# Batch 0 of an attention + FFN kernel: FFN1 of quad 0 placed ahead of quad 1's, in other PSUM banks; one load moved, one square moved to ScalarE

## The chip, the cores and the metric

One core of a Trainium2 chip. The metric is the device time of one execution in microseconds, the median over the runs. Besides it, every run has a span: the time from the first to the last record of the core's engines. Each ratio below is of runs in the fast state, made in the same rounds on the same chip.

## The reference

```python
def _attn_ref(q, k, v):                      # q, k, v: (8, 12, 448, 64)
    S = q.shape[2]
    scores = np.matmul(q, k.transpose(0, 1, 3, 2)) / np.sqrt(q.shape[-1])
    attn = np.maximum(scores, 0.0) ** 2 / S
    return np.matmul(attn, v)

def _moe_ref(x, w_in, w_out, alpha):         # x: (3584, 768); w_in: (768, 2048); w_out: (2048, 768)
    h = x @ w_in
    g = np.maximum(h, 0.0) + alpha * np.minimum(h, 0.0)
    return g @ w_out
```

The attention output, with its heads side by side, is x. All is float32 outside; the kernel computes with bfloat16 operands.

## The kernel before

Heads are taken four at a time: a "quad" is four heads of one batch, and three quads make one batch. A quad's scores come in seven chunks (`j` from 0 to 6). Each chunk is four matmuls on 64 x 64 quadrants of TensorE, a relu out of PSUM, and a square (two chunks per instruction on VectorE; a seventh chunk alone is the "single" square). Then follows the product with v (`attnv`), whose result is copied to `xT`. FFN1 (`ffn1`) needs all three quads of a batch: inputs `km` 0 and 1 come from quad 0, 2 and 3 from quad 1, 4 and 5 from quad 2.

PSUM is divided into two double buffers (`sc_ps`) and four single banks (`mm_ps`) that rotate. Score chunks use either; FFN1 accumulators use single banks.

```python
    sc_ps = pool("scps", 2, **PSUM)          # tiles [128, 2, 512] float32
    mm_ps = pool("mmps", 4, **PSUM)          # tiles of one bank

    def attnv(n, js=range(NJ), space=sc_ps, apart=False):
        if js[0] == 0:
            if space is mm_ps:
                av_ps[n] = [mm_ps.tile([128, 512], F32, ...) for _ in range(2)]
            elif apart:                      # each half in a double buffer of its own
                av_ps[n] = [sc_ps.tile([128, 2, 512], F32, ...)[:, 0] for _ in range(2)]
            else:
                av_ps[n] = sc_ps.tile([128, 2, 512], F32, ...)
        ...
        for j in js:
            a = att.pop((n, j))
            for r in range(2):
                for s in range(2):
                    nc.tensor.matmul(half[r][64 * s:64 * s + 64, :S], ...)
        ...                                  # batch 0: half 0 copied by ScalarE, half 1 by VectorE (g > 0)

    def ffn1(b, ff, kms=range(KM)):
        if kms[0] == 0:
            hps[ff] = mm_ps.tile([128, S], F32, ...)
        ...                                  # one matmul per km
        nc.scalar.activation(neg, ps, ACTF.Relu, scale=-1.0)
        nc.vector.scalar_tensor_tensor(gT..., neg, beta..., ps, ALU.mult, ALU.add)

    for n in range(NG):                      # batch 0
        last = n == NG - 1
        for j in range(NJ):
            ...
            if j == 2 or j == (4 if last else 5):
                scores(n, j, "both", mm_ps)
            else:
                scores(n, j, "act")
            ...
            if j == 3 and n > 0:
                attnv(n - 1, space=mm_ps)
            ...
            if last and j > 4:
                ffn1(0, j - 5, range(0, 4))
            if last and j == 6:
                ffn1(0, 2, range(0, 4))
        if n == 0:
            load_bf16(2)                     # k, q, v of quad 2
            load_w_in(0, 512)                # four transfers
            load_w_in(512, 1024)
            load_w_in(1024, 2048)
            load_bf16(3)
    ...
    squares(single=nc.vector)
    attnv(2, range(0, 4), apart=True)
    attnv(2, range(4, NJ))
    ffn1(0, 3, range(0, 4))
    ...
    for ff in range(4):
        ffn1(0, ff, range(4, KM))
```

Below, AV1 and AV2 are `attnv` of quads 1 and 2, and "step 4" of FFN1 is its `ff` 4.

## Time and profile before

| | before |
|---|---|
| time, median of the first 3 runs (range) | 390.79 us (390.65 to 391.74) |
| TensorE busy | 379.5 us of a 389.6 us span |
| TensorE's waits after 20 us | 0.38 + 0.21 us |
| AV1's first matmul | 19.74 us |
| AV1's first matmul to the first FFN1 matmul after AV2 | 6.56 us |
| AV1's first matmul to the first FFN2 matmul | 25.66 us |
| first FFN2 matmul to the end of the span | 344.21 us |

### The profile page before, as it was taken

What the parts mean: (1) busy time and instruction counts of PE and PEld (TensorE: products, weight loads), DVE (VectorE), ACT (ScalarE), POOL (GpSimd) and SP (SyncE); (2) the same over time, 40 slices, a digit from 0 to 9 for tenths busy, and PEclk for the clock granted to TensorE, in tenths of its full rate; (3) what the DMA queues carried; (4) which work ended last, traced back from release to release, by engine and by line L of the source; (5) the groups of instructions that cost most, each with busy time, mean ns of one, the idle gap of its engine ahead of it and who ended that gap; (6) DMA issues with size and microseconds to landing.
All of it is one profiled execution on the core that took longest, in us unless ns stands there. A gap on an engine that the chain in (4) does not pass through costs nothing.

```text
span 389.6 us, 7873 instructions
## 1 busy us (share of the span) xinstructions
PE 379.5 (97%) x3210; PEld 214.8 (55%) x3210; DVE 253.2 (65%) x336; ACT 215.5 (55%) x361; POOL 74.9 (19%) x89
## 2 busy tenths in 40 slices
PE   6799999999999999999999999999999999999996
PEld 4345556545655456645665456654566545655564
DVE  4986877687687757766675666777676376726411
ACT  5965767464566656664473645756565366624200
POOL 7654000052251114201221012301030000000000
PEclk9999999999999999999999999999999999999999
DMA  8999997894995519825494354937253220130033
GB/s 163 191 209 204 204 216 264 235 300 100 259 258 182 126 65 240 222 65 164 94 260 150 67 164 98 278 126 174 29 91 87 70 47 2 42 81 2 0 82 81
DMA packets 64755, 55.43 MB, mean 142 GB/s; under 512 B 35776, under 2 KB 60496, under 8 KB 64720
## 3 DMA queue, kind: packets, MB, share of 16 engines
q1 hardware_dynamic: 53504, 44.78, 44.7%
q0 software_dynamic: 10976, 9.96, 16.1%
q8 instruction: 25, 0.41, 0.4%
q10 hardware_dynamic: 240, 0.20, 0.2%
q14 instruction: 10, 0.08, 0.1%
HBM read 45.62 MB, written 11.01 MB: 145 GB/s over the span
## 4 chain that ended last, share of the span: by engine, by line
PE 93%; ACT 2%; DMA 2%; DVE 1%; POOL 1%; issue 0%; POOLq 0%; DVEq 0%
PE hps L255 37%; PE ops L271 37%; PE avh L223 7%; PE sc L156 6%; PE sch L156 3%; DMA qe<-in_q_dram 2%; PE ops L294 1%; PE av L223 1%; PE tps L131 1%; ACT rl L185 1%; DVE at L196 1%; ACT xT L232 0%; POOL ke L357 0%; POOL ke L355 0%; POOL qe L355 0%
## 5 line engine op out<-in xcount | busy, mean ns | idle before, releaser
L255 PE MATMUL hps<-xT,w_in_sb 128*128 128x448 bf16 x768 | 149.2, 353 | 0.6 <-ACT xT L232 0.4
L271 PE MATMUL ops<-w_out_sb,gT 128*128 128x384 bf16 x864 | 145.8, 326 | 0.0
L263 DVE SCALAR_TENSOR_TENSOR gT<-neg,beta_sb,hps 128x448 bf16<-128x448 f32 x128 | 85.7, 679 | 58.3 <-ACT neg L262 57.5
L271 PEld LDWEIGHTS <-gT 128*128 128x128 bf16 x864 | 83.4, 98 | 61.2 <-issue 7.9
L255 PEld LDWEIGHTS <-w_in_sb 128*128 128x128 bf16 x768 | 74.0, 98 | 72.5 <-issue 5.5
L262 ACT ACTIVATE neg<-hps 128x448 f32<-128x448 f32 x128 | 69.1, 546 | 63.7 <-PE hps L255 63.6
L185 ACT ACTIVATE rl<-sc 128x896 bf16<-128x896 f32 x87 | 77.1, 923 | 44.1 <-PE sc L156 44.0
L196 DVE TENSOR_TENSOR at<-rl 128x1792 bf16<-128x1792 bf16 x80 | 85.7, 1113 | 2.1 <-ACT rl L185 0.9
L106 DVE COPY osb<-ops 128x384 f32<-128x384 f32 x30 | 16.7, 557 | 45.6 <-PE ops L271 45.6
L163 ACT ACTIVATE rl<-sch 128x448 bf16<-128x448 f32 x81 | 41.6, 550 | 4.7 <-PE sch L156 4.6
L106 POOL CAST kb<-kraw 128x896 bf16<-128x896 f32 x16 | 18.8, 1178 | 114.5 <-DMA kT<-kb 55.9
L156 PE MATMUL sc<-qT,kT 64*64 64x448 bf16 x456 | 36.1, 355 | 3.1 <-ACT rl L185 1.4
L223 PE MATMUL avh<-at,vb 64*64 64x448 bf16 x588 | 34.4, 350 | 0.4 <-DVE at L196 0.4
L156 PEld LDWEIGHTS <-kT 64*64 64x64 bf16 x672 | 21.8, 106 | 19.6 <-issue 13.2
L104 ACT COPY osb<-ops 128x384 f32<-128x384 f32 x24 | 11.4, 476 | 36.0 <-PE ops L271 36.0
L223 PEld LDWEIGHTS <-vb 64*64 64x64 bf16 x672 | 25.7, 106 | 9.8 <-issue 5.2
L183 DVE TENSOR_SCALAR rl<-sc 128x896 bf16<-128x896 f32 x27 | 29.4, 1089 | 0.6 <-PE sc L156 0.6
L106 POOL CAST vb<-vraw 128x896 bf16<-128x896 f32 x16 | 15.9, 991 | 36.8 <-PE avh L223 36.7
L106 POOL CAST qb<-qraw 128x896 bf16<-128x896 f32 x16 | 16.6, 1040 | 32.3 <-DMA qT<-qb 28.0
L156 PE MATMUL sch<-qT,kT 64*64 64x448 bf16 x216 | 22.5, 355 | 0.0
L165 DVE TENSOR_SCALAR rl<-sch 128x448 bf16<-128x448 f32 x27 | 16.8, 622 | 2.8 <-PE sch L156 0.8
L238 DVE TENSOR_SCALAR xT<-avh 128x448 bf16<-128x448 f32 x19 | 11.9, 624 | 7.7 <-PE avh L223 7.7
(59 smaller groups left out, 98.4 us busy)
## 6 DMA issues: line engine op xcount, KB each, us to landing
out_dram<-osb SPq DMA_DIRECT2D x54, 192.0 KB, 2.8
qraw<-in_q_dram SPq DMA_DIRECT2D x19, 448.0 KB, 5.3
kraw<-in_k_dram SPq DMA_DIRECT2D x18, 448.0 KB, 4.4
vraw<-in_v_dram SPq DMA_DIRECT2D x18, 448.0 KB, 6.1
w_out_sb<-in_moe_w_out_dram POOLq DMA_DIRECT2D x2, 1536.0 KB, 20.0
w_in_sb<-in_moe_w_in_dram POOLq DMA_DIRECT2D x8, 192.0 KB, 8.7
w_in_sb<-in_moe_w_in_dram POOLq DMA_DIRECT2D x4, 384.0 KB, 9.8
vb<-in_v_dram POOLq DMA_DIRECT2D x6, 224.0 KB, 9.6
```

Source lines behind the costliest of these rows:

```text
L106: eng.tensor_copy(o, i)
L156: nc.tensor.matmul(half[r][64 * c:64 * c + 64, :S], kT[n][64 * r:64 * r + 64, j, c, :], qT[n][64 * r:64 * r + 64, :, c, :], start=True, st ...
L163: nc.scalar.activation(rl[:, r], half[r][:, :S], ACTF.Relu)
L165: nc.vector.tensor_scalar(rl[:, r], half[r][:, :S], 0.0, None, ALU.max)
L183: nc.vector.tensor_scalar(rl, ps[:, :, :S], 0.0, None, ALU.max)
L185: nc.scalar.activation(rl, ps[:, :, :S], ACTF.Relu)
L196: nc.vector.tensor_tensor(a, t, t, ALU.mult)
L223: nc.tensor.matmul(half[r][64 * s:64 * s + 64, :S], vb[n][64 * r:64 * r + 64, s, j, :], a[64 * r:64 * r + 64, s], start=(j == 0), stop=(j ...
L255: nc.tensor.matmul(ps, w_in_sb[:, km // 2, km % 2, bass.ts(ff, 128)], xT[b][:, km // 2, km % 2, :], start=(km == 0), stop=(km == KM - 1))
L262: nc.scalar.activation(neg, ps, ACTF.Relu, scale=-1.0)
L263: nc.vector.scalar_tensor_tensor(gT[b // 2][:, ff, (b % 2) * S:(b % 2) * S + S], neg, beta_sb[:, ff:ff + 1], ps, ALU.mult, ALU.add)
L271: nc.tensor.matmul(ps, gT[sb][:, ff, bass.ts(c, 128)], w_out_sb[:, ff, bass.ts(hf, 384)], start=(ff == 0), stop=(ff == KF - 1))
```

## The change

Its intent is to remove TensorE's wait for a PSUM bank before the first FFN1 matmul. Chunk 4 of quad 2 no longer takes two single banks, so that FFN1's first accumulators find the banks of chunk 2 free. The matmuls of quad 0, which is ready early, then go ahead of those of quad 1. The first columns of w_in, now needed earlier, are loaded ahead of quad 2's v, and the single square goes to ScalarE.

```diff
@@ batch 0, scores
-            if j == 2 or j == (4 if last else 5):
+            if last and j == 4:
+                scores(n, j, "both")
+            elif j == 2 or j == 5 and not last:
                 scores(n, j, "both", mm_ps)
@@ batch 0, FFN1
-            if last and j > 4:
-                ffn1(0, j - 5, range(0, 4))
+            if last and j == 4:
+                ffn1(0, 0, range(0, 2))
+                ffn1(0, 1, range(0, 2))
+            if last and j == 5:
+                ffn1(0, 0, range(2, 4))
+                ffn1(0, 1, range(2, 4))
             if last and j == 6:
                 ffn1(0, 2, range(0, 4))
         if n == 0:
-            load_bf16(2)
+            load_bf16(2, "kq")
             load_w_in(0, 512)
+            load_bf16(2, "v")
             load_w_in(512, 1024)
@@ after batch 0's scores
-    squares(single=nc.vector)
+    squares(single=nc.scalar)
     attnv(2, range(0, 4), apart=True)
```

## The prediction

> **What bounds the kernel now.** I first read the page: busy shares, slices, chain.
>
> ```profile
> span 389.6 us, 7873 instructions
> PE 379.5 (97%) x3210; PEld 214.8 (55%) x3210; DVE 253.2 (65%) x336; ACT 215.5 (55%) x361; POOL 74.9 (19%) x89
> ...
> PEclk9999999999999999999999999999999999999999
> ...
> PE 93%; ACT 2%; DMA 2%; DVE 1%; POOL 1%; issue 0%; POOLq 0%; DVEq 0%
> ```
>
> TensorE is busy for 97% of the span and carries 93% of the chain, at full clock. All TensorE idle time together is about 10 us (389.6 minus 379.5). The change touches only batch 0, so I took TensorE's waits from 18 to 40 us:
>
> ```profile
> PE sc L156 <- DVE qT L106: 0.6, 1, 0.6
> PE sc L156 <- ACT rl L185: 0.6, 2, 0.3
> PE hps L255 <- ACT xT L232: 0.4, 1, 0.4
> PE hps L255 <- DVE gT L263: 0.2, 1, 0.2
> ```
>
> The first two lie before 19.6 us, ahead of the changed code. Only the other two, 0.6 us, are in its reach. From 30 us to the end TensorE waits for nothing. The TensorE timeline gives the order (columns: start, duration, engine, line, operation, idle before with its releaser):
>
> ```profile
> 19.74 1.52 PE L223 MATMUL avh<-at,vb 64*64 64x448 bf16 x28
> 21.06 0.42 PE L156 MATMUL sch<-qT,kT 64*64 64x448 bf16 x4
> 21.25 0.42 PE L156 MATMUL sc<-qT,kT 64*64 64x448 bf16 x4
> 22.05 0.94 PE L255 MATMUL hps<-xT,w_in_sb 128*128 128x448 bf16 x4 [0.38 <-ACT xT L232]
> 22.92 0.38 PE L156 MATMUL sc<-qT,kT 64*64 64x448 bf16 x4
> 23.23 1.69 PE L255 MATMUL hps<-xT,w_in_sb 128*128 128x448 bf16 x8
> 24.85 1.52 PE L223 MATMUL av<-at,vb 64*64 64x448 bf16 x28
> 26.30 2.44 PE L255 MATMUL hps<-xT,w_in_sb 128*128 128x448 bf16 x12
> 28.96 0.35 PE L255 MATMUL hps<-xT,w_in_sb 128*128 128x448 bf16 x1 [0.21 <-DVE gT L263]
> ```
>
> The first FFN1 matmul (hps) follows chunks 4 (sch) and 5 (sc) of quad 2 and starts at 22.05, when ScalarE has copied quad 1's half 0 out of avh (xT, 21.37 to 22.00). It needs only quad 0, ready since 16.6 (the copies at 15.66 and 16.10 took 0.54 each). It waits for its bank: the four single banks rotate (avh takes two, sch of chunk 4 two), so the next tile gets a bank that avh still holds. That is the wait the change attacks.
>
> **What the Trainium skill says.**
> 1. "Perfetto Trace Analysis", Optimization Strategy: find the gaps of the engine that bounds the regime and what semaphore ends them. The trace agrees that this is the place to look, but the gaps here come to 0.6 us in 389.6.
> 2. "ScalarE: Activation LUTs", What ACT_TABLE_LOAD costs: an ACTIVATE with immediate scale and bias takes 186 + 0.833 N ns. For N = 896 that is an estimate of 932 ns; the trace has 923 (relu) and 950 (the Squares it already runs). Agrees. It counts a load for a switch of table sets; the trace shows one load in all, with Relu, Copy and Square running after it, so I add none.
> 3. "DMA: Bandwidth & Descriptors", Issuing engines are not separate DMA queues: all transfers run on the same 16 engines. Moving v behind w_in thus adds no bandwidth, it changes an order. The trace agrees so far as POOL's issues wait in turn for earlier landings.
> 4. "PSUM — Partial Sum Buffer", The four PSUM rules: one matmul output stays within a 2 KiB bank. Chunks of 448 float32 columns are 1,792 bytes, one bank each, as the pools have it; the trace has no row on the bank size itself.
>
> **The change part by part.**
>
> (a) *Banks.* Chunk 4 moves from two single banks to one double score buffer. The first two hps tiles then take chunk 2's banks, whose relus ended at 20.75 (ScalarE, 20.15 + 0.60) and 21.06 (VectorE, 20.44 + 0.62). Chunk 4 takes the buffer of chunk 1, whose relu is over by about 20.3; chunk 5 that of chunk 3 (over at 20.57 + 0.99 = 21.56); chunk 6 now that of chunk 4, whose VectorE half ended at 22.50 + 0.61 = 23.11.
>
> (b) *Order.* The build shows the new TensorE order: chunk 4, four hps matmuls of quad 0 (ff 0 and 1), chunk 5, four of quad 1, chunk 6, four for ff 2, attention of quad 2 (AV2). The same matmuls as before, so no work is removed. Two durations from the timeline: a chunk between FFN1 groups takes 23.23 - 22.92 = 0.31; four FFN1 matmuls up to the next chunk take 22.92 - 22.05 = 0.87. Walking from the end of AV1 at 21.06:
> - chunk 4 at 21.06, hps quad 0 at 21.37,
> - chunk 5 at 22.24 (21.56 is past),
> - hps quad 1 at 22.55; its first input is ready at 22.00, its second at 21.97 + 0.62 = 22.59, and it comes second, at about 22.75,
> - chunk 6 at 23.42 (23.11 is past),
> - hps ff 2 at 23.73, AV2 at 24.60.
>
> Against 24.85 that is 0.25 us: the stall of nearly 0.5 (21.56 to 22.05 in starts) goes, and one more switch between 64-row chunks and full FFN1 matmuls (0.31 instead of the 0.19 that chunk 4 took, and some 0.06 at the end of an FFN1 group, plus rounding) takes about half of it back.
>
> (c) *The wait that takes its place.* AV2 puts its second half into the buffer of chunk 6, so its third matmul needs chunk 6's relu. Elsewhere in the trace a relu starts 0.45 after its chunk (16.07 to 16.52), takes 0.92, and releases TensorE 0.04 later: 1.41 us. Before, eight FFN1 matmuls followed chunk 6 and hid this (22.92 + 1.41 = 24.33, before 24.85; ScalarE in fact ended at 24.27). Now only four follow: 23.42 + 1.41 = 24.83. The third matmul of AV2 stood at about 24.95 before (two at 0.05, from 28 in 1.45). **The gain shrinks from 0.25 to 0.12 us.**
>
> (d) *The last square.* It leaves VectorE (0.62 us, 25.04 to 25.66) and costs 0.95 on ScalarE. There it starts when chunk 6's relu is over, about 24.82, ending near 25.77. AV2's first use of it is its 25th matmul, 24.83 + 22 x 0.052 = 25.97. VectorE still squares chunks 4 and 5 until 25.12, for the 17th matmul at 25.56. ScalarE's next task, the xT copy, begins after AV2, above 26.2. Off the path by about 0.2 us: worth nothing, costing nothing.
>
> (e) *v behind w_in.* POOL's waits show one eight-deep order: issue n waits for landing n - 8. From it, quad 2's v landed at 17.2 and the four first w_in pieces by about 18.0, 18.9, 20.2 and 21.2. The first hps now starts at 21.37 and its second matmul needs the last piece: in the old order that is a margin of about 0.3 us. In the new order w_in moves one place up (some 2 us earlier), and v lands about 21.2, needed at 24.6. It is insurance for (a), not a gain itself.
>
> (f) *The second gap.* The fifth hps tile takes the first one's bank, after its last matmul (ending 27.62), neg (0.55), gT (0.69) and hand-overs, to 28.96. The order and banks there are the same in the new build, so this 0.2 stays, moved with the rest.
>
> **Sum:** 0.38 us of attacked wait, about 0.13 back to switching, about 0.13 to the relu of chunk 6: **0.12 us gained of 390.8.**
>
> **Rivals.**
> - *All of the gap is gained.* If relu 6 ends sooner or chunk 6 is issued sooner than I walk it, up to 0.4 us, 390.4. For it: the stall is real and on the chain. Against it: the relu's 1.41 us is longer than the 0.31 + 0.87 of work now beside it.
> - *A wait takes its place wholly.* The square on ScalarE is 0.33 longer than on VectorE, with 0.2 of slack; if it slips, or chunk 5's or 6's buffers come free late, AV2 stalls for 0.2 to 0.5: 390.8 to 391.1. Against it: each hand-over above is met by 0.1 us or more.
> - *A transfer becomes the bound.* The last w_in column block, for ff 8, has to be there at about 33.8; POOL's wait for it ended at 32.98. Starting 0.1 sooner leaves 0.7 us. v two microseconds later meets 3 us of slack. If a landing shifts by more than that, 391.5. The new order moves no transfer after the first w_in pieces, so I give this little.
> - *TensorE's load afterwards swallows nothing.* From 30 us it never waits, so what is gained by 29 us should reach the end. The chance that a later stage gives it back is small.
>
> **Range and chances.** The measure is 390.79 (390.65 to 391.74); 390.79 - 0.12 gives **390.7 us**. The three runs before lie 1.1 us apart, more than the effect. I choose 390.0 to 391.3: the low end has the full 0.6 us of reachable gaps and a little luck, the high end a new 0.5 us stall or a median among slower runs. Two per cent is 7.8 us; the whole idle time of TensorE is 10 us, and 0.6 of it in reach. So the chance of faster by over 2% is 0.01, slower 0.01, **within 2% 0.98**.
>
> **What would show it.** In the profile after, the 0.38 wait of hps for xT should be gone, with the first hps near 21.4 (a); chunk 6 near 23.4 and AV2 near 24.6 (b); a new small wait of AV2 (av) for ScalarE's relu, 0.1 to 0.2 us (c); a Square of 0.95 us on ScalarE near 24.8 with nobody waiting for it (d); no wait for w_in or vb on TensorE (e); the 0.2 wait for gT still there, near 28.8 (f). TensorE's busy time should stay near 379.5. A first hps held by w_in, a wait of AV2 for the square, or a new wait behind 30 us would each make the prediction wrong; so would a drift between measurements larger than the change.

## The result, and the profile after

| | before | changed |
|---|---|---|
| time, median (range), 6 runs each | 390.92 us (390.50 to 391.74) | 391.19 us (390.95 to 391.39) |
| ratio changed / before | | 1.0005 (0.9992 to 1.0018) |
| AV1's first matmul | 19.74 us | 19.06 us |
| AV1 to FFN1 after AV2 | 6.56 us | 6.53 us |
| AV1 to the first FFN2 matmul | 25.66 us | 25.98 us |
| first FFN2 matmul to the end | 344.21 us | 344.22 us |

A ratio is the mean time of one kernel's fast runs over that of the other's in the same rounds, so it is not quite the ratio of the medians. The interval contains 1, and 391.19 lies in the predicted range of 390.0 to 391.3. The trace shows what cancels.

The first lines of the page of the changed kernel, and its chain:

```profile
span 389.3 us, 7871 instructions
PE 380.3 (98%) x3210; PEld 215.2 (55%) x3210; DVE 252.8 (65%) x335; ACT 216.2 (56%) x362; POOL 76.2 (20%) x89
...
PE 91%; DMA 6%; POOL 1%; DVE 0%; issue 0%; ACT 0%
```

The engines' busy times are nearly the same as before. The chain differs: 6% of it now runs through transfers instead of 2%. TensorE's waits from 18 to 40 us in the changed kernel say where:

```profile
PE sc L156 <- ACT rl L185: 0.6, 2, 0.3
PE hps L255 <- DVE gT L263: 0.2, 1, 0.2
PE hps L255 <- DMA w_in_sb<-in_moe_w_in_dram: 0.2, 1, 0.2
```

The 0.38 us wait of hps for xT is gone, and a wait for w_in stands in the list. TensorE's timeline of the changed kernel (start, duration, engine, line, operation, idle before):

```profile
19.06 1.52 PE L223 MATMUL avh<-at,vb 64*64 64x448 bf16 x28
20.38 0.39 PE L156 MATMUL sc<-qT,kT 64*64 64x448 bf16 x4
20.70 0.93 PE L255 MATMUL hps<-xT,w_in_sb 128*128 128x448 bf16 x4
21.56 0.38 PE L156 MATMUL sc<-qT,kT 64*64 64x448 bf16 x4
21.88 0.93 PE L255 MATMUL hps<-xT,w_in_sb 128*128 128x448 bf16 x4
22.74 0.38 PE L156 MATMUL sc<-qT,kT 64*64 64x448 bf16 x4
23.05 0.93 PE L255 MATMUL hps<-xT,w_in_sb 128*128 128x448 bf16 x4
23.91 1.74 PE L223 MATMUL av<-at,vb 64*64 64x448 bf16 x28
25.59 2.44 PE L255 MATMUL hps<-xT,w_in_sb 128*128 128x448 bf16 x12
28.24 4.89 PE L255 MATMUL hps<-xT,w_in_sb 128*128 128x448 bf16 x25 [0.21 <-DVE gT L263]
33.32 1.10 PE L255 MATMUL hps<-xT,w_in_sb 128*128 128x448 bf16 x5 [0.19 <-DMA w_in_sb<-in_moe_w_in_dram]
```

Three things are to be seen here.

1. From AV1 to AV2 it is 23.914 - 19.058 = 4.86 us instead of 24.849 - 19.742 = 5.11. The predicted 0.25 us is there.
2. AV2 then takes 1.67 us to the next FFN1 matmul instead of 1.45, which gives 0.22 back. No idle time is printed in front of it. The wait sits inside AV2, where the views of idle time do not show it, because two of AV2's matmuls are already running. It counts as busy time, as the extra switching does: in the 25.6 us from AV1 on, TensorE is busy for 25.01 us before and for 25.39 us in the second profile of the changed kernel (the last experiment, without a wait for w_in), for the same matmuls.
3. The second matmul of FFN1 step 8, at 33.32, waited for w_in. It began 0.54 us after the first instead of 0.19, so this cost 0.35 us (the 0.19 printed is only the part with no matmul running).

Narrow windows make the second point visible; the line of `av` in each is shown. First the kernel before from 24.84 to 25.00, then the changed one from 23.9 to 24.1 and from 24.1 to 24.2.

```profile
24.85 0.38 PE L223 MATMUL av<-at,vb 64*64 64x448 bf16 x4
```

```profile
23.91 0.38 PE L223 MATMUL av<-at,vb 64*64 64x448 bf16 x2
23.91 0.61 PE L223 MATMUL av<-at,vb 64*64 64x448 bf16 x6
```

Before, four matmuls, one on each quadrant, begin together (24.849, 24.852, 24.856 and 24.859 us). The Trainium skill, "TensorE: Matmul & The Clock Gate", The mechanism of Part 3, states a distance of about 4 ns between such starts; the trace has 3 to 4. In the changed kernel only two begin, at 23.914 and 23.917. The third, the first into chunk 6's buffer, begins at 24.142, and three more follow it within 0.01 us. ScalarE's timeline of the changed kernel has the reason:

```profile
22.00 0.92 ACT L185 ACTIVATE rl<-sc 128x896 bf16<-128x896 f32 x1 [0.25 <-PE sc L156]
23.17 0.92 ACT L185 ACTIVATE rl<-sc 128x896 bf16<-128x896 f32 x1 [0.26 <-PE sc L156]
24.12 0.95 ACT L200 ACTIVATE at<-rl 128x896 bf16<-128x896 bf16 x1
```

The second line is chunk 6's relu, and it ends at 24.09, 0.051 us before AV2's third matmul. The third is the moved square.

Two things meet in the third point. AV1 began 0.68 us sooner in this profile, for reasons that lie before the changed code (the kernel before waited 0.67 us for k of quad 1, the changed kernel's profile did not). And the last block of w_in landed at 33.18 us, the latest of all profiles that load it as one block (31.62 to 33.18); it was needed at 32.97. How far such scatter goes was a question for the experiments.

### The profile page after: what moved, and what is told of

The parts are those of the page before. It is cut to its first block, busy times and chain, and to the rows that moved or that the text cites. A ratio compares the mean times of both kernels' runs of the same rounds, so it can differ in the third digit from the quotient of the medians.

```text
span 389.3 us, 7871 instructions
## 1 busy us (share of the span) xinstructions
PE 380.3 (98%) x3210; PEld 215.2 (55%) x3210; DVE 252.8 (65%) x335; ACT 216.2 (56%) x362; POOL 76.2 (20%) x89
## 4 chain that ended last, share of the span: by engine, by line
PE 91%; DMA 6%; POOL 1%; DVE 0%; issue 0%; ACT 0%
PE ops L271 37%; PE hps L255 35%; PE avh L223 7%; PE sc L156 6%; DMA w_in_sb<-in_moe_w_in_dram 3%; PE sch L156 3%; DMA vb<-in_v_dram 2%; PE ops L294 1%; PE tps L131 1%; DMA qraw<-in_q_dram 1%; PE av L223 1%; POOL w_in_sb L141 1%; POOL ke L100 0%; POOL qe L100 0%; DVE rl L165 0%
## 5 line engine op out<-in xcount | busy, mean ns | idle before, releaser
L106 POOL CAST kb<-kraw 128x896 bf16<-128x896 f32 x16 | 20.5, 1283 | 111.2 <-DMA kT<-kb 53.6
L106 POOL CAST qb<-qraw 128x896 bf16<-128x896 f32 x16 | 15.8, 990 | 32.5 <-DMA qT<-qb 28.8
```

Source lines behind the costliest of these rows:

```text
L106: eng.tensor_copy(o, i)
```

## The experiments

**The theory** to be tested: the change removes 0.25 us of stall ahead of AV2 and pays 0.22 back inside AV2 for chunk 6's relu; the square and the move of v are off the path; the w_in wait is scatter of a landing that lies close behind TensorE. **The rivals**: the square on ScalarE is what AV2 waits for; or the order of the loads causes the shifts; or something further on gives the gain back.

All stage times are from the starts of matmuls in each kernel's one profile; the profiles come from several chips. The last column is the median, over a kernel's runs, of time minus span.

| kernel | AV1 starts | AV1 to FFN1 after AV2 | AV1 to FFN2 | FFN2 to end | time minus span |
|---|---|---|---|---|---|
| before | 19.74 | 6.56 | 25.66 | 344.21 | 1.86 |
| before again | 19.11 | 6.56 | 25.67 | 344.19 | 1.87 |
| only v moved | 18.77 | 6.56 | 25.67 | 344.18 | 1.88 |
| only order and banks | 19.70 | 6.54 | 25.64 | 344.18 | 2.15 |
| changed | 19.06 | 6.53 | 25.98 | 344.22 | 2.15 |
| changed again | 19.19 | 6.53 | 25.63 | 344.20 | 2.12 |
| square back on VectorE | 19.06 | 6.53 | 25.63 | 344.21 | 2.15 |
| v first again | 19.10 | 6.52 | 25.63 | 344.21 | 2.12 |
| one FFN1 matmul ahead | 19.16 | 6.53 | 25.67 | 344.23 | 2.10 |
| AV2 in one buffer | 18.98 | 6.38 | 25.89 | 344.22 | 2.12 |
| w_in split | 19.16 | 6.53 | 25.80 | 344.19 | 2.12 |
| one ahead and split | 19.59 | 6.53 | 25.53 | 344.18 | 2.14 |
| eight matmuls left out | 19.25 | 6.53 | 25.52 | 344.60 | 2.13 |
| eight left out, w_in split | 18.99 | 6.53 | 24.98 | 344.20 | 2.08 |

All kernels but the last two, which compute a wrong result on purpose, were correct. The column "FFN2 to end" answers the third rival: apart from one of these two, it stays between 344.18 and 344.23, so nothing is given back behind the first FFN2 matmul.

### The square back on VectorE

```diff
-    squares(single=nc.scalar)
+    squares(single=nc.vector)
     attnv(2, range(0, 4), apart=True)
```

> The change with its last odd square put back on VectorE, all else kept. Theory (AV2 of quad 2 is held only by the relu of chunk 6): the distance from AV2's first matmul to the next FFN1 matmul stays 1.67 us as in the changed kernel (1.45 before), time within 0.3 us of it. Rival (the 0.95 us square on ScalarE is what AV2 waits for): the distance falls to 1.45 and the profile loses 0.2 us.

Measured: 391.10 us, ratio to before 1.0006 (0.9993 to 1.002). AV2 is still 1.67 us long, to 0.01. VectorE's timeline shows the square there, between the pair squares and the copy of AV2's second half:

```profile
22.35 2.08 DVE L196 TENSOR_TENSOR at<-rl 128x1792 bf16<-128x1792 bf16 x2
24.36 0.62 DVE L202 TENSOR_TENSOR at<-rl 128x896 bf16<-128x896 bf16 x1
25.69 0.62 DVE L234 TENSOR_SCALAR xT<-av 128x448 bf16<-128x448 f32 x1 [0.71 <-PE av L223]
```

The square ended at 24.98 here and at 24.12 + 0.95 = 25.07 on ScalarE, and AV2's matmuls stand at the same places both times, to 0.01 us. The rival that AV2 waits for the square falls. But the square on ScalarE has no slack left. AV2's 25th matmul, the first to use it, begins 1.208 us after AV2's first, 0.050 us after the square's end; with the square on VectorE it begins at 1.204. So it just binds, at a cost of 0.004 us.

### v first again

```diff
-            load_bf16(2, "kq")
+            load_bf16(2)
             load_w_in(0, 512)
-            load_bf16(2, "v")
             load_w_in(512, 1024)
```

> The change with v of quad 2 loaded ahead of w_in again. Theory (moving v only buys margin): w_in's first four pieces land near 18.0, 18.9, 20.2 and 21.2 us; the first FFN1 group stands at about 21.4 minus whatever the start ran early, so it waits 0 to 0.4 us for w_in, none in a run whose attention of quad 1 starts at 19.7, some 0.3 in one that starts at 19.1. Rival (v's place matters nowhere): no wait in either case. Time within 0.4 us of the changed kernel.

Measured: 391.09 us, ratio 1.0004 (0.999 to 1.0018). No wait for w_in, although AV1 began at 19.10. I had expected about 0.3 us of wait there; the pieces landed sooner than in the kernel before, the fourth by 20.55, when POOL's wait for it ended, against a need at 20.94. So the landings differ from run to run, and I had taken one profile's for fixed.

### One FFN1 matmul ahead of AV2

```diff
+    ffn1(0, 3, range(0, 1))
     attnv(2, range(0, 4), apart=True)
     attnv(2, range(4, NJ))
-    ffn1(0, 3, range(0, 4))
+    ffn1(0, 3, range(1, 4))
```

> The change with one FFN1 matmul of ff 3 issued ahead of AV2 instead of after it (same work). Theory (AV2's third matmul waits 0.23 us for chunk 6's relu): 0.19 us of that is filled, AV2's first matmul to the next FFN1 matmul falls from 1.67 to about 1.48, and from quad 1's attention to the twelfth FFN1 matmul after AV2 0.19 us are won. Rival (the wait is the square's, or the copy of quad 2 then holds the fifth FFN1 matmul): 1.67 stays, or a new wait of up to 0.2 for the copy xT appears. Time 0 to 0.2 us less than the changed kernel, not resolvable by the clock, so the trace decides.

Measured: AV2 1.48 us (1.67 before the edit), as the theory says. Its third matmul is 0.038 us behind the first, where it was 0.228: 0.19 us of other work put ahead of it takes 0.19 off, as it must where the wait ends at a fixed time. That this time is the end of chunk 6's relu is shown by the distance: in all ten profiles with the new order and AV2 in two buffers, this one among them, the third matmul begins 0.051 to 0.052 us after that relu ends. But only 0.10 of it is kept at FFN1 step 4 (9.08 us after AV1 instead of 9.18), because the copy xT now holds the fourth FFN1 matmul after AV2 for 0.09 (its start 0.276 us after the third's instead of 0.189). And step 8 lost 0.15 to w_in in this profile. The time, 391.20 us (ratio 1.0006, 0.9993 to 1.002), resolves none of it.

### AV2 in one double buffer

```diff
-    attnv(2, range(0, 4), apart=True)
+    attnv(2, range(0, 4))
```

> The change with both halves of AV2 in one double buffer, that of chunk 5, so that it no longer needs chunk 6's relu. Theory: the 0.23 us wait inside AV2 is gone (1.45 us from its first matmul to the next FFN1), but VectorE's copy now waits for ScalarE's copy of the same tile (the build shows that wait), so the FFN1 matmul that needs half 1 stalls for about 0.3 us: the total is the same or 0.1 worse. Rival (the relu is not what holds AV2): 1.67 stays.

Measured: the wait for chunk 6's relu is gone (the third matmul begins 0.007 us after the first), AV2 takes 1.52 us. The first six passes are spaced as before the change and the last one is 0.05 us late: it waited for the square on ScalarE, which ended at 24.05 + 0.95 = 25.00. Then came the expected new wait, in TensorE's waits from 20 to 60 us:

```profile
PE hps L255 <- DVE xT L234: 0.2, 1, 0.2
PE hps L255 <- DVE gT L263: 0.2, 1, 0.2
```

Start to start the first costs 0.602 - 0.189 = 0.41 us. AV1 to FFN2 is 25.89 us, 0.26 worse than the changed kernel without a w_in wait; I had expected up to 0.1. By the clock it is 391.28 us, ratio 1.0009 (0.9995 to 1.0023). The two separate buffers earn their place; the wait for the relu is their price.

### w_in's last block split

```diff
-            load_w_in(1024, 2048)
+            load_w_in(1024, 1536)
+            load_w_in(1536, 2048)
```

> The change with w_in's last 1,024 columns loaded as two blocks of 512 (same bytes). Theory (the 0.19 us wait of FFN1 step 8 is for the end of that block, which lands near 33.2 us however early TensorE is): the columns of step 8 land some 3 to 7 us sooner, no wait for w_in at step 8, 0.2 us won in a run that starts early, nothing in one that starts late. Rival (the wait is for something else that ends then): it stays. Risk: four more issues push k of quad 3 later, a new wait of its transpose near 34.4.

Measured: 391.29 us, ratio 1.0012 (0.9999 to 1.0026). Step 8 does not wait for w_in: its second matmul begins the regular 0.19 us after the first. But the transposes of quad 3's k, right after step 8, come 1.40 us after its start instead of 1.23. The risk that I had named is the result here: k is issued four places later, lands at 34.23 and is 0.17 us late; the transposes begin at 34.28.

### One ahead and split together

> One FFN1 matmul ahead of AV2 and w_in's last block split, together: the candidate. Theory: both waits gone, 0.2 to 0.4 us less than the changed kernel in the trace from quad 1's attention to FFN2; by the clock 390.8 against 391.0 to 391.2, likely unresolved. Rival (time is given back later): the distance from FFN1 step 9 to the end grows by the same amount.

Its edits are those of the last and the third experiment. Measured: AV1 to FFN2 in 25.53 us, the best of all correct kernels, 0.14 less than before the change and 0.10 less than the changed kernel without a w_in wait (I had expected 0.2 to 0.4), and the rest of the kernel keeps its 344.18. A part of this is the late start of this profile, at 19.59: k of quad 3 landed at 34.10 and was used at 34.43; with a start at 19.06 it would have been needed at 33.90. By the clock it is 391.14 us, ratio 1.0006 (0.9993 to 1.0018): no version that can be told from the kernel before.

### Eight FFN1 matmuls left out

```diff
         for km in kms:
+            if b == 0 and 4 <= ff < 8 and km in (2, 3):
+                continue
             nc.tensor.matmul(ps, w_in_sb[...], ...)
```

> Wrong result on purpose: the change with eight FFN1 matmuls left out (two each of steps 4 to 7 of batch 0), 1.51 us of TensorE work ahead of step 8. Theory (w_in's last block caps what can be won before 33.2 us): step 8 waits about 1.2 to 1.7 us for w_in, and the time falls by only 0 to 0.5 us. Rival (the path is TensorE alone): no longer wait, time falls by 1.5 us.

This asks how much time could be won at all ahead of step 8. Measured: 390.54 us against 390.94, ratio 0.9995 (0.9978 to 1.0011), for 1.51 us of work less. TensorE's waits from 20 to 60 us:

```profile
PE hps L257 <- DMA w_in_sb<-in_moe_w_in_dram: 0.9, 1, 0.9
PE tps L131 <- DMA qe<-in_q_dram: 0.2, 1, 0.2
PE hps L257 <- DVE gT L265: 0.2, 1, 0.2
PE ops L273 <- DMA w_out_sb<-in_moe_w_out_dram: 0.2, 1, 0.2
```

Step 8's second matmul began 1.27 us after the first instead of 0.19, so w_in alone took 1.08 of the 1.51 (expected: 1.2 to 1.7). Further transfers, w_out and a q, then held TensorE as well. The cap is shown for this profile: with 1.5 us less of work, TensorE meets one transfer after the other.

### Eight left out, w_in split

The edit of the last experiment and the split of w_in's last block together.

> Wrong result on purpose: the eight matmuls left out and w_in's last block split. Theory: step 8 no longer waits, and 1.0 to 1.5 us of the 1.51 reach the end, less what k of quad 3 (needed by its transpose one step later) may then hold. Rival (something other than w_in's block caps it): as the run without the split, 0 to 0.5 us.

Measured: AV1 to FFN2 in 24.98 us, 0.65 less than the changed kernel without a w_in wait. The wait moved to the next transfer:

```profile
PE tps L131 <- DMA ke<-in_k_dram: 0.8, 1, 0.8
PE hps L257 <- DMA w_in_sb<-in_moe_w_in_dram: 0.2, 1, 0.2
```

That is less than the 1.0 to 1.5 us that I expected to reach the end, and for the named reason, k of quad 3. The times do not settle the size: 391.00 us in the median of 4 runs from 390.27 to 391.70, ratio 1.001 (0.9994 to 1.0025).

### The kernel before against itself

> The kernel before, unchanged, run as the candidate against itself. All eight variants so far show 2.06 to 2.18 us between the clock and the span of the core's records, the kernel before 1.81 to 1.91. Theory (the 0.25 us belongs to the program): here it is 1.87 on both sides. Rival (it belongs to the place in the round): 2.13 for this copy. Its profile is the second of the kernel before: from quad 1's attention to the first FFN2 matmul 25.6 to 25.7 us, and a start of that attention anywhere from 19.0 to 19.8.

This run was a control. Every variant of the change had shown 2.06 to 2.18 us between time and span, and the kernel before 1.81 to 1.91, on both chips used by then. Was it the place in the round? Measured: 391.16 against 391.09 us, ratio 0.9999 (0.9978 to 1.0021), and 1.83 to 1.91 us outside the span for the copy too. It is not the place in the round; it belongs to the program. The stages repeat to 0.01 us (6.56 and 25.67), while AV1 began at 19.11 instead of 19.74.

### Order and banks alone

The changed kernel with both other edits undone (square on VectorE, v first).

> The new order and banks alone: square on VectorE and v ahead of w_in as before. Theory: it is the whole of the change for TensorE, so 6.53 us from quad 1's attention to the FFN1 run after AV2 (6.56 before), AV2 stretched to 1.67, and outside the span 2.13 if the extra 0.25 belongs to the reordered program. Rival (v or the square makes the shift): 1.87 outside the span.

Measured: 6.54 and 25.64 us, AV2 1.67, and 2.10 to 2.19 us outside the span; 391.33 us, ratio 1.0002 (0.9982 to 1.0022). The reorder alone carries the whole of the change, in the stages and outside the span. In this profile the second FFN1 matmul began 0.215 us after the first, where 0.200 is usual: the fourth piece of w_in had only just landed. So the move of v buys margin that is sometimes needed, here by 0.015 us.

### Only v moved

The kernel before with the load order of the change.

> The kernel before with only v of quad 2 moved behind w_in's first columns. Theory: nothing changes for TensorE: first FFN1 matmul 2.31 us after quad 1's attention began, held by the copy xT (0.38 idle), AV2 1.45, time as before; w_in's first pieces land 1 to 1.5 us sooner. Rival (the order of loads drives the small shift): 0.2 us and more in the span, or 2.13 outside it.

Measured: 391.10 us against 391.09, ratio 0.9993 (0.9968 to 1.0018). TensorE's timeline stands as before, shifted as a whole by the early start:

```profile
18.77 1.52 PE L223 MATMUL avh<-at,vb 64*64 64x448 bf16 x28
...
21.07 0.94 PE L255 MATMUL hps<-xT,w_in_sb 128*128 128x448 bf16 x4 [0.38 <-ACT xT L232]
...
23.88 1.52 PE L223 MATMUL av<-at,vb 64*64 64x448 bf16 x28
25.33 2.44 PE L255 MATMUL hps<-xT,w_in_sb 128*128 128x448 bf16 x12
```

The wait of 0.38 for the copy xT is there, 1.88 us lie outside the span, and the rival that the order of the loads drives the shift falls.

### The changed kernel once more

> The changed kernel, unchanged, once more. Theory (the 0.35 us that step 8 lost to w_in in its first profile is scatter of the landing, 31.9 to 33.5 us over the runs): lost only if the landing comes later than 13.9 us after quad 1's attention began; the sum of start, stages and tail explains the span to 0.1 us. Rival (it belongs to the change): it is there again with a landing before that.

Measured: AV1 to FFN2 in 25.63 us, with no wait for w_in; POOL's wait for the last piece ended at 32.58, and step 8's second matmul came at 33.10. The 0.35 us of the first profile did not recur. It is scatter, and it fits the expectation: there the wait had ended at 33.47 by POOL, after 19.06 + 13.91 = 32.97. The other correct kernels that load the block as one fit it too: where it landed by 32.76 nobody waited for it, and one FFN1 matmul ahead, where it landed at 32.98, lost 0.15 us. The median of 391.99 us contains two runs of 392.76 and 392.93 at a granted clock of 0.996; the kernel before had 392.13 and 393.25, at 0.996 and 0.990, in the same session. I draw nothing from them.

## Why the prediction was right, step by step

The time was right: 390.7 us predicted, 391.19 measured, inside 390.0 to 391.3, and "within 2%". Within 2% was well founded, by the 0.6 us of idle time in reach. That the median lies inside the narrower range owes more to luck: the range is ten times as wide as the forecast gain of 0.12 us, the measured medians differ by 0.27 us the other way, and a difference of that size lies outside the span, which the prediction didn't consider (last point below). Two of the signs by which it wanted to be called wrong did appear: a new wait behind 30 us, for w_in, in one of two profiles, and a drift between measurements as large as the change (the median of the kernel before went from 390.79 to 390.92). TensorE's busy time, which should have stayed near 379.5, was 380.3; that says little, since a second profile of the kernel before has 380.0. Its steps:

- **(a), banks**: right. The first hps begins 20.70 - 19.06 = 1.64 us after AV1 instead of 2.31, and waits for nothing.
- **(b), order**: right. 0.25 us predicted up to AV2's start, 0.25 measured (5.11 to 4.86); with 0.38 us of idle gone, the extra switching cost that it had counted took back about what it said.
- **(c), the wait that takes its place**: the mechanism was right, the size was off. The term was "two at 0.05, from 28 in 1.45", which let two of AV2's matmuls run alone for 0.1 us and left 0.13 of wait. The trace shows four matmuls starting within 0.01 us and one such pass each 0.19. Two that start alone win nothing, because the second half still has its own seven passes to run, so the wait counts from AV2's start: 24.142 - 23.914 = 0.23 us, of which 0.22 show in AV2's length. The relu's end itself was predicted well: AV2's third matmul begins 5.08 us after AV1's first, against 24.83 - 19.74 = 5.09. An average spacing was taken for the spacing of single instructions.
- **The sum**: 0.12 predicted; 0.02 to 0.04 us measured to the FFN2 matmuls (25.63 and 25.64 against 25.66 and 25.67). As predicted, what is gained by then is not given back later.
- **(d), the square**: right that it costs nothing, wrong on why. The slack of "about 0.2" is not there. The square ends 1.16 us after AV2's start, as predicted (25.77 - 24.60 = 1.17), but AV2's 25th matmul was put at 25.97, which is 1.37 after AV2's start, again by the average spacing. It begins at 1.204 where the square is done early, because only AV2's second half is late and the first half nearly keeps its pace (1.159 before). With the square on ScalarE it begins at 1.208, 0.050 us after the square's end. In the single-buffer variant, where the first half isn't late at all, the same square costs 0.05.
- **(e), v**: right as insurance; of the two reordered kernels' profiles without it, one needed it, by 0.015 us. w_in's four first pieces came 1.2 to 1.5 us sooner in the changed kernel's first profile, not "some 2". (The landings that the prediction reads from POOL's waits are 0.3 us late throughout: by the trace the four pieces landed at 17.7, 18.7, 19.9 and 20.9.)
- **(f), the second gap**: right, 0.21 us in both kernels.
- **The rival of the transfers**: "I give this little" was too little. It took 0.35 us in one of the two profiles of the changed kernel. The margin of 0.7 us was read from one profile, and slightly wrong: the block was needed at 33.68 there, not "about 33.8". And the scatter of the start (AV1 from 18.77 to 19.74 over 14 profiles) and of the landing (31.62 to 33.18) is larger than the margin.
- **Not foreseen at all**: 0.26 us outside the span. Medians of the span are equal: 389.1 us over 35 runs of the kernel before and 389.1 over 10 of the changed one. The clock's 0.2 us of difference (391.01 to 391.22 over the same runs) is time minus span, 1.86 against 2.14. It comes with the reordered program, in all eleven sets of runs with the reorder (2.06 to 2.19 us) and in none without it (1.81 to 1.91). Over all runs the medians are 1.87 and 2.13. No record shows what it is, so its cause stays open; the traces end alike (the last DMA packet ends 1.69 to 1.74 us before the end of the span in every profile).

## What to carry to other kernels

Where one engine is busy for 97% of the span, sum up its idle time that the change can reach before anything else: here 0.6 us of 390 bounded what an edit that takes no work away could gain. A wait that is removed by issuing something sooner tends to reappear at the next buffer whose release hangs on a fixed latency; count the work that is left beside that latency (here four matmuls instead of eight). And read margins to transfers from several profiles, since two profiles of one kernel differ here by more than the change is worth.

## What the Trainium skill lacked or had wrong

- "TensorE: Matmul & The Clock Gate", Part 3: the 4 ns between tiles is right (3 to 4 ns here), and the matmuls' start in program order is stated. What it does not draw from this is the cost when a pack of four is half blocked: the two that could start gained nothing, and AV2 grew from 1.45 to 1.67 us for a release 0.23 us late.
- "TensorEngine Tiling (Array Packing)", Key Properties, says that changing the tiling mode drains TensorE, without a figure. Here a chunk of four 64 x 64 matmuls followed by full ones took 0.31 us up to the next matmul, and 0.19 when more 64 x 64 work followed it, so about 0.12 us for the way to full tiles. The way back cost about 0.09: 0.28 us from the last full matmul to AV2's first (23.632 to 23.914). That the drain is what takes this time is not shown.
- "Perfetto Trace Analysis", Optimization Strategy, has one look for the gaps between slices. The wait that the change itself brought, 0.23 us, made no gap: two matmuls of the same pack covered it. It shows only in the length of a group (1.67 against 1.45 us).
- No page that I read has that the time outside the first and the last record can differ between two programs of almost the same instructions: 1.87 us before, 2.13 us with the reorder.
